# A retention layer that feeds a token-mixing layer on one core: instructions put in another order, three more transposes by DMA, and sums in two PSUM banks at the end

## The chip, the core and the metric

The kernel runs on one core of a Trainium2 chip. That core has five engines, each of which works through its own list of instructions in order: TensorE (PE in the profile; PEld is its loading of weights), VectorE (DVE), ScalarE (ACT), GpSimd (POOL) and SyncE (SP, which issues the DMA transfers here). They wait for each other through semaphores. Matrix products are written to PSUM, a memory in banks, from which DVE and ACT read them here. The metric is the device time of one execution in microseconds (us).

## The reference, cut to what matters

```python
# retention: q, k, v of [4 batches, 8 heads, 768 tokens, 64]
for t in range(S):
    state = gamma[None, :, None, None] * state + np.einsum('bhd,bhe->bhde', k[:, :, t], v[:, :, t])
    y[:, :, t] = scale * np.einsum('bhd,bhde->bhe', q[:, :, t], state)
x = np.ascontiguousarray(attn_out.transpose(0, 2, 1, 3)).reshape(B, S, H * D)   # [4, 768, 512]
# mixing
theta = x @ w_theta
cos_t, sin_t = (np.cos(theta), np.sin(theta))
zr = x * cos_t
zi = x * sin_t
yr = np.einsum('ts,bsd->btd', w_tok_r, zr)
yi = np.einsum('ts,bsd->btd', w_tok_i, zi)
y = yr + yi
u = x + y
return (u + np.maximum(u @ w_ch, 0.0))
```

## The kernel before, in words

**Tiles.** The 768 tokens of a batch are six tiles of 128. The retention takes them two at a time: a *pair* n (0 to 11, three to a batch) covers 256 tokens as two interleaved chunks of 128. The mixing takes the 24 tiles one at a time and calls them m (0 to 23, six to a batch).

**A pair.** `prep` scales and casts k (ACT), q and v (POOL, in the first pairs partly DVE) to bf16. `flip` turns k and q round with eight PE transposes each into one PSUM bank, and DVE copies that bank out (L186); `flip_dma` does the same by one DMA transpose. `ret_A` multiplies k and q, `ret_mask` masks the product (DVE, L211), `ret_Y` multiplies it with v, `ret_I` adds the part that comes from the state. `ret_S` adds k and v to the state in PSUM and ends with two ACT copies that put the state into `stbd` for the next `ret_I` (L266). `ret_out` copies the pair's x, still transposed, out of PSUM (two ACT copies, L275). `x_pe` or `x_dma` turns x round. `theta` makes x @ w_theta for one chunk (four PE matmuls) and lets ACT take cosine and sine (L299, L300); `zmul` multiplies both with x (DVE, L306).

**A tile.** `moe_M` sums twelve matmuls, two for each of six steps s0 (step s0 needs z of chunk s0 of the batch), into one bank `y_ps`. `moe_u` adds x to it (DVE, L325). `moe_U` (PE transposes, ACT copy) or `moe_U_dma` turns u round, `moe_O` makes u @ w_ch (four matmuls), `moe_out` finishes (DVE, L353), `store` writes out.

**PSUM banks** are handed out by tag: `y` has one bank, `tr` two (all transposes and `o_ps` in turn), `acc` two (the two `yT_ps` of a pair, then the two `th_ps`, and so on in turn), `at` and `st` hold the masked product and the state. A new user of a bank waits until its last reader is through.

**Order.** Nothing is scheduled by a planner: `manual_schedule` leaves each engine's instructions in the order in which the code is written. A prologue (L441 to L537) handles pairs 0 to 2, with `keep_busy` matmuls that do no work of the reference. Then *slot* n = 3 to 12 (L547 on) does the first half of pair n, the second half of pair n - 1, the tiles `tiles_of[n]` (one tile in slots 3 to 6, two from slot 7 on), and the `moe_O` of the slot before. `w_cast` and `w_tok` cast and transpose one row block of the token weights. After slot 12 come tiles 18 to 22 one by one, and `moe_last` for tile 23.

**Loads.** SP issues the loads of pairs 0 to 5 and all weights at the start, in the order of L111, as buffers come free. The loads of pair n + 3 are issued in slot n, in SP's order behind what stands before them: `x_dma`, `flip_dma`, `moe_U_dma` and the stores are issued by SP too.

**What the change touches.** In `ret_S` the state copies (L264 to L266). In the slot: the DMA limit for k and q (`KQ_DMA`, L63 and L550), the places of `moe_U_dma` (L556), `w_cast(4)` (L565), `theta` and `x_pe` (L586 to L589), the split of the first tile's products at `part` (L583), the flips (L593), `w_tok` (L600, L619), and the order of `moe_M`, `moe_u`, `zmul` and `moe_O` at the slot's end (L612 to L628). The tag of `y_ps` (L314), the last lines of the prologue and the loop of the last tiles.

Of the kernel before, what the change touches and what calls it, by code (L numbers as in the profile page):

```python
# [14 lines left out]
FT = mybir.dt.float32  # L15
# [17 lines left out]
def kernel(  # L33
# [18 lines left out]
    B, H, S, D = q.shape  # L52
    dm = H * D
# [191 lines left out]
    def ret_S(n, a):  # L245

        b, g = divmod(n, nG)
        c = 2 * g + a
        if c == nT - 1:
            return  # L250
        half = slice(a * HP, (a + 1) * HP)
        if c == 0:
            st_ps[b] = psum.tile([P, NP, D], FT, name="st_ps", tag="st", bufs=1)
        for two in range(2):
            for j in range(NP):
                for par in range(2):
                    h = 2 * j + par
                    nc.tensor.matmul(st_ps[b][par * D:(par + 1) * D, j, :],  # L258
                                     st[n, "k"][half, two, h * D:(h + 1) * D],
                                     st[n, "v"][half, two, h * D:(h + 1) * D],  # L260
                                     start=(c == 0 and two == 0 and j == 0),
                                     stop=(c == nT - 2 and two == 1 and j == NP - 1),
                                     skip_group_check=True)
        for par in range(2):  # L264
            sl = slice(par * D, (par + 1) * D)
            nc.scalar.copy(stbd[(c + 1) % 2][sl, :, sl], st_ps[b][sl])  # L266
# [184 lines left out]
    ret_mask(0, 0)  # L451
    keep_busy(2)
    ret_S(0, 0)
    keep_busy(1)
    ret_A(0, 1)
    ret_mask(0, 1)
    ret_S(0, 1)
    ret_Y(0, 0)
    ret_I(0, 1)
    keep_busy(3)  # L460
# [16 lines left out]
    ret_mask(1, 0)  # L477
    keep_busy(2)
    ret_S(1, 0)
    ret_A(1, 1)  # L480
    ret_mask(1, 1)
    prep(2, "k", K)
    ret_Y(1, 0)
    ret_I(1, 0)
    ret_S(1, 1)
    ret_I(1, 1)
    keep_busy(2)
    zmul(0, 0)
# [16 lines left out]
    theta(1, 1)  # L505
    x_pe(1, 1, 2)
    ret_S(2, 0)
    ret_A(2, 1)
    ret_mask(2, 1)
    ret_Y(2, 0)  # L510
# [24 lines left out]
    flip(3, "q")  # L535
    prep(4, "k", K)
    w_cast(3)  # L537


    tiles_of = {nG - 2: [], nG - 1: [0, 1]}  # L540
# [6 lines left out]
    for n in range(nG, B * nG + 1):  # L547
        mine, done = tiles_of[n], tiles_of[n - 1]
        late, two = n > nG, len(mine) > 1
        q_dma = n + 1 >= KQ_DMA  # L550
# [9 lines left out]
        if n + 1 in pairs:  # L560
            prep(n + 1, "q", PP)
            prep(n + 1, "v", PP)
        if n == nG:
            nc.gpsimd.tensor_copy(wch, wdma["ch"])
            w_cast(4)  # L565
        if n == nG + 1:
            w_cast(5)
        if late:
# [24 lines left out]
        if n + 1 in pairs:  # L593
            if q_dma:
                flip_dma(n + 1, "q")
            else:
                flip(n + 1, "k")
                flip(n + 1, "q")
        if n == nG:
            w_tok(3)  # L600
        if n + 3 in pairs:
            load(n + 3, "v")
        for t in tiles_of[n - 2]:
            store(t)

        if n in pairs:
            ret_S(n, 0)
            ret_A(n, 1)
            ret_mask(n, 1)
            ret_Y(n, 0)  # L610
            ret_I(n, 0)
        if n < U_DMA:  # L612
            moe_U(done)
        if two:
            moe_M(mine[1], 0, nT)
        else:
            moe_M(mine[0], part, nT)
        if n in (nG, nG + 1):
            w_tok(n - nG + 4)  # L619
# [12 lines left out]
    for m in range(last_m - nT + 1, last_m):  # L632
        if m - 1 > last_m - nT:
            moe_U_dma(m - 1)
        else:
            moe_U_dma(m - 2)
            moe_U_dma(m - 1)
        moe_M(m, 0, nT)
        moe_u(m)
# [8 lines left out]
_INS = ['q', 'k', 'v', 'moe_w_theta', 'moe_w_tok_r', 'moe_w_tok_i', 'moe_w_ch']  # L648
# [26 lines left out]
```

## Time and profile before

| what | value |
|---|---|
| time, median of 13 runs | 180.96 us (180.09 to 183.65) |
| time of the profiled execution | 180.96 us |
| its span | 179.3 us |
| PE busy | 162.5 us, 91% of the span |
| DVE, ACT, POOL busy | 103.7, 82.7, 63.2 us |
| read from HBM, written to it | 25.69 MB, 6.29 MB |

The span is the stretch from the first to the last instruction; the 1.7 us between it and the time lie outside of what the profile shows. A line of the profile gives a start in us from the span's start and a duration. In square brackets stands how long the engine had been idle before that instruction, and what ended the wait. A matmul's row is longer than its share of the engine, since the next one starts while it drains; so a short wait of PE shows less idle time than it costs. In this trace, slots 3 to 12 begin at about 43.3, 53.6, 65.1, 75.5, 84.3, 95.5, 107.7, 118.6, 129.9 and 141.2 us, and the last tiles at 151.4.

### The profile page before, as it was taken

Reading aid. Unit: us, or ns where it says so; the run is one execution under the profiler, and the core shown is the slowest. Engines: PE = TensorE matmul, PEld = TensorE weight load, DVE = VectorE, ACT = ScalarE, POOL = GpSimd, SP = SyncE. Lnnn points to the kernel's source line nnn. Section 1 sums busy time; section 2 is a strip of 40 time slices with the busy share of each in tenths; the row PEclk is TensorE's granted clock in tenths of the full one; section 3 lists DMA queues with packets and bytes.
Section 4 is the critical chain, followed back from the end, with each engine's and each line's share of the span. In section 5 each row is a group of like instructions: output and inputs, shape, how many; then the busy total and the mean of one; then the engine's idle time right before and its main releaser. Section 6 shows DMA issues by size and latency. Waiting matters only on the chain.

```text
span 179.3 us, 4745 instructions
## 1 busy us (share of the span) xinstructions
PE 162.5 (91%) x2003; PEld 90.3 (50%) x2003; DVE 103.7 (58%) x142; ACT 82.7 (46%) x141; POOL 63.2 (35%) x81
## 2 busy tenths in 40 slices
PE   7689898977798997999999999999999989999990
PEld 2355565544544654655465645454455434444560
DVE  2366798775644674969297474672746535334441
ACT  7236494932356658575773744728055250000010
POOL 5284656492996856802718063000000000000000
PEclk9999999999999999999999999999999999999999
DMA  4999999999999999339696596765719162353343
GB/s 137 311 328 332 295 316 331 347 343 282 321 335 295 291 305 314 122 65 286 162 252 185 120 263 124 200 119 102 165 29 208 29 176 58 138 148 100 88 146 119
DMA packets 63621, 37.13 MB, mean 207 GB/s; under 512 B 20976, under 2 KB 58096, under 8 KB 63600
## 3 DMA queue, kind: packets, MB, share of 16 engines
q1 hardware_dynamic: 63456, 36.71, 76.0%
q8 instruction: 15, 0.25, 0.6%
q10 hardware_dynamic: 144, 0.13, 0.2%
q14 instruction: 6, 0.05, 0.1%
HBM read 25.69 MB, written 6.29 MB: 178 GB/s over the span
## 4 chain that ended last, share of the span: by engine, by line
PE 67%; ACT 8%; DMA 8%; DVE 6%; issue 5%; POOL 3%; DVEq 0%; ACTq 0%; POOLq 0%
PE y_ps L318 27%; PE o_ps L346 11%; PE th_ps L296 10%; DMA pair<-in_q_dram 6%; PE kq_ps L183 3%; PE yT_ps L227 3%; ACT cs L300 3%; PE at_ps L204 3%; PE yT_ps L241 3%; DMA pair<-in_k_dram 2%; PE st_ps L258 2%; ACT cs L299 2%; PE y_ps L392 2%; DVE z L306 1%; DVE at L211 1%
## 5 line engine op out<-in xcount | busy, mean ns | idle before, releaser
L318 PE MATMUL y_ps<-z,wtr 128*128 128x512 bf16 x138 | 52.4, 380 | 1.5 <-DVE u L325 1.0
L318 PE MATMUL y_ps<-z,wti 128*128 128x512 bf16 x138 | 52.4, 379 | 0.0
L325 DVE TENSOR_TENSOR u<-y_ps,x_sb 128x512 bf16<-128x512 f32 x23 | 15.9, 690 | 39.7 <-PE y_ps L318 39.6
L175 POOL TENSOR_TENSOR kqb<-pair,qscp 128x512 bf16<-128x512 f32 x20 | 22.0, 1115 | 38.1 <-DMA pair<-in_q_dram 31.0
L211 DVE TENSOR_TENSOR at<-at_ps,maskp 128x1024 bf16<-128x1024 f32 x24 | 29.3, 1220 | 4.1 <-PE at_ps L204 4.1
L266 ACT CAST stbd<-st_ps 64x256 bf16<-64x256 f32 x40 | 14.6, 365 | 27.2 <-PE st_ps L258 26.7
L175 POOL TENSOR_TENSOR kqb<-pair,vscp 128x512 bf16<-128x512 f32 x24 | 25.4, 1079 | 3.6 <-DMA pair<-in_v_dram 1.9
L296 PE MATMUL th_ps<-wth,xT 128*128 128x512 bf16 x96 | 23.2, 380 | 1.4 <-ACT xT L275 1.3
L346 PE MATMUL o_ps<-wch,uT 128*128 128x512 bf16 x92 | 22.8, 379 | 0.3 <-DVE wtr L378 0.3
L318 PEld LDWEIGHTS <-wti 128*128 128x128 bf16 x138 | 13.5, 98 | 16.0 <-issue 3.1
L299 ACT ACTIVATE cs<-th_ps,halfpi 128x512 bf16<-128x512 f32 x24 | 16.5, 689 | 10.1 <-PE th_ps L296 10.1
L318 PEld LDWEIGHTS <-wtr 128*128 128x128 bf16 x138 | 13.4, 97 | 14.4
L275 ACT CAST xT<-yT_ps 128x512 bf16<-128x512 f32 x22 | 15.0, 737 | 11.1 <-PE yT_ps L227 10.9
L186 DVE COPY kqT<-kq_ps 128x1024 bf16<-128x1024 bf16 x20 | 13.5, 687 | 9.2 <-PE kq_ps L183 9.0
L353 DVE SCALAR_TENSOR_TENSOR ot<-o_ps,u 128x512 f32<-128x512 f32 x23 | 15.9, 691 | 4.8 <-PE o_ps L346 4.6
L306 DVE TENSOR_TENSOR z<-cs,x_sb 128x1024 bf16<-128x1024 bf16 x24 | 17.6, 772 | 0.5 <-DMA x_sb<-xT 0.4
L300 ACT ACTIVATE cs<-th_ps,zerob 128x512 bf16<-128x512 f32 x24 | 16.5, 688 | 0.0
L183 PE MATMUL kq_ps<-ident,kqb 128*128 128x128 bf16 x160 | 11.8, 219 | 4.0 <-DVE kqb L175 1.0
L169 ACT CAST kqb<-pair 128x1024 bf16<-128x1024 f32 x12 | 12.6, 1048 | 5.5 <-DMA pair<-in_k_dram 5.4
L296 PEld LDWEIGHTS <-xT 128*128 128x128 bf16 x96 | 8.6, 97 | 12.4 <-ACT xT L275 3.7
L346 PEld LDWEIGHTS <-uT 128*128 128x128 bf16 x92 | 8.9, 97 | 10.7 <-issue 0.7
L183 PEld LDWEIGHTS <-kqb 128*128 128x128 bf16 x160 | 9.9, 98 | 7.7 <-issue 2.4
(57 smaller groups left out, 155.7 us busy)
## 6 DMA issues: line engine op xcount, KB each, us to landing
pair<-in_k_dram SPq DMA_DIRECT2D x12, 512.0 KB, 6.7
pair<-in_q_dram SPq DMA_DIRECT2D x12, 512.0 KB, 7.6
pair<-in_v_dram SPq DMA_DIRECT2D x12, 512.0 KB, 8.0
out_dram<-ot SPq DMA_DIRECT2D x23, 256.0 KB, 2.6
wtok<-in_moe_w_tok_r_dram SPq DMA_DIRECT2D x6, 384.0 KB, 6.5
wtok<-in_moe_w_tok_i_dram SPq DMA_DIRECT2D x6, 384.0 KB, 6.3
w<-in_moe_w_theta_dram SPq DMA_DIRECT2D x1, 1024.0 KB, 8.1
w<-in_moe_w_ch_dram SPq DMA_DIRECT2D x1, 1024.0 KB, 8.9
```

What stands on the lines that cost most here:

```text
L175: engines[two].tensor_mul(dst[:, two], src[:, two], _bcast_last(sc[:, 2 * g + two], D))
L183: nc.tensor.transpose(ps[:, two, j, :], st[n, name][:, two, j * P:(j + 1) * P], ident)
L211: nc.vector.tensor_mul(at.rearrange("p a j t -> p (a j) t"), at_ps.rearrange("p a j t -> p (a j) t"), _bcast_mid(maskp[:, two].rearrange(" ...
L275: copy(st[n, "xT"][:, a].rearrange("e j (i w) -> e j w i", w=2), st[n, "y"][a].rearrange("e j (w i) -> e j w i", w=2))
L296: nc.tensor.matmul(th_ps, st[n, "xT"][:, a, j, :], wth[:, j, :], start=(j == 0), stop=(j == NP - 1))
L299: nc.scalar.activation(cs[:, 0, :], th_ps, AF.Sin, bias=halfpi, scale=1.0)
L300: nc.scalar.activation(cs[:, 1, :], th_ps, AF.Sin, bias=zerob, scale=1.0)
L306: nc.vector.tensor_mul(zs[b][:, c], st[n, "cs", a], _bcast_mid(xs[b][:, c, :], 2))
L318: nc.tensor.matmul(y_ps, wT[r][:, s0, t0 * P:(t0 + 1) * P], zs[b][:, s0, r, :], start=(s0 == 0 and r == 0), stop=(s0 == nT - 1 and r == 1))
L325: nc.vector.tensor_add(u, mo[m]["y"], xs[b][:, t0, :])
L346: nc.tensor.matmul(o_ps, mo[m]["uT"][:, j, :], wch[:, j, :], start=(j == 0), stop=(j == nD - 1))
L353: nc.vector.scalar_tensor_tensor(ot, mo[m]["o"], 0.0, mo[m]["u"], ALU.max, ALU.add)
```

## The change

- **State copies.** They leave `ret_S` and become `state_out`. Everywhere but in one place it is called right behind `ret_S`, so nothing moves there. In the slot, for pair n - 1, it is called behind the two `ret_out`.
- **k by DMA.** `flip` of k becomes `flip_dma` for pairs 7, 8 and 9 too (slots 6, 7 and 8); q stays with PE up to pair 9.
- **Products.** The first of two tiles is split after three steps in place of four, around the two `theta`. Of a single tile the steps 2 and 3 come before the `w_tok`, the steps 4 and 5 behind it (in slot 6 the steps 2 and 3 come right behind the flip). `x_pe` stands between the two `theta`.
- **u.** The `moe_u` of a single tile comes before `zmul`. From slot 8 on, the first tile's `moe_U_dma` is issued in its own slot.
- **Weights.** `w_tok(2)` and `w_tok(3)` move up in the prologue, the second from slot 3; `flip(3, "k")`, `flip(3, "q")` stand inside products; `w_cast(4)` goes ahead of the cast of w_ch on POOL.
- **The end.** From tile 17 on `y_ps` takes the two banks of `acc` in turn. In slot 12 the second tile comes behind both `moe_O`; in tiles 18 to 22 `moe_O` stands between the steps 3 and 4.

```diff
-    KQ_DMA, X_DMA, U_DMA = 3 * nG + 1, 2 * nG - 1, 3 * nG
+    K_DMA, Q_DMA, X_DMA, U_DMA = 2 * nG + 1, 3 * nG + 1, 2 * nG - 1, 3 * nG
...
+    def state_out(n, a):
+        b, g = divmod(n, nG)
+        c = 2 * g + a
+        if c == nT - 1:
+            return
         for par in range(2):
             sl = slice(par * D, (par + 1) * D)
             nc.scalar.copy(stbd[(c + 1) % 2][sl, :, sl], st_ps[b][sl])
...
-            mo[m] = dict(y=psum.tile([P, dm], FT, name="y_ps", tag="y", bufs=1))
+            if m < (B - 1) * nT - 1:
+                y_ps = psum.tile([P, dm], FT, name="y_ps", tag="y", bufs=1)
+            else:
+                y_ps = psum.tile([P, dm], FT, name="y_ps", tag="acc", bufs=2)
+            mo[m] = dict(y=y_ps)
...
     moe_M(0, 2, 4)
     zmul(2, 0)
     prep(3, "k", K)
+    w_tok(2)
+    moe_M(0, 4, 5)
     zmul(2, 1)
-    moe_M(0, 4, nT)
+    flip(3, "k")
+    moe_M(0, 5, nT)
     moe_u(0)
     prep(3, "q", DP)
     prep(3, "v", PP)
-    w_tok(2)
-    flip(3, "k")
-    moe_M(1, 0, nT)
+    w_cast(3)
+    moe_M(1, 0, 4)
+    flip(3, "q")
+    moe_M(1, 4, nT)
     moe_u(1)
-    flip(3, "q")
+    w_tok(3)
     prep(4, "k", K)
-    w_cast(3)
...
-        if n + 1 in pairs and q_dma:
+        nxt = n + 1 in pairs
+
+        if nxt and n + 1 >= K_DMA:
             flip_dma(n + 1, "k")
         if n + 3 in pairs:
             load(n + 3, "k")
         if n >= U_DMA:
-            for t in done:
-                moe_U_dma(t)
+            moe_U_dma(done[1])
...
             ret_S(n - 1, 1)
             ret_out(n - 1, 0, nc.scalar.copy)
             ret_out(n - 1, 1, nc.scalar.copy)
+            state_out(n - 1, 1)
...
-        part = 4 if two else 2
-        moe_M(mine[0], 0, part)
+        first = mine[0]
+        moe_M(first, 0, 3 if two else 2)
         if late:
             theta(n - 1, 0)
-            theta(n - 1, 1)
             if n - 1 < X_DMA:
                 x_pe(n - 1)
+            theta(n - 1, 1)
         if two:
-            moe_M(mine[0], part, nT)
-            moe_u(mine[0])
...
+            moe_M(first, 3, nT)
+            moe_u(first)
+        for name, limit in (("k", K_DMA), ("q", Q_DMA)):
+            if nxt and n + 1 < limit:
+                flip(n + 1, name)
+        if not two and n + 1 >= K_DMA:
+            moe_M(first, 2, 4)
+        if nxt and n + 1 >= Q_DMA:
+            flip_dma(n + 1, "q")
...
+        if n + 1 >= U_DMA:
+            moe_U_dma(first)
...
-        if two:
+        if not two:
+            if n + 1 < K_DMA:
+                moe_M(first, 2, 4)
+            if n in (nG, nG + 1):
+                w_tok(n - nG + 4)
+            moe_M(first, 4, nT)
+            moe_u(first)
+        elif n in pairs:
             moe_M(mine[1], 0, nT)
...
         if late:
             zmul(n - 1, 0)
             zmul(n - 1, 1)
-        moe_u(mine[-1])
+        if two and n in pairs:
+            moe_u(mine[1])
         for t in done:
             moe_O(t)
             moe_out(t)
+        if n not in pairs:
+            moe_M(mine[1], 0, nT)
+            moe_u(mine[1])
...
     for m in range(last_m - nT + 1, last_m):
...
+        moe_U_dma(m - 1)
+        moe_M(m, 0, 4)
...
         moe_O(m - 2)
         moe_out(m - 2)
         store(m - 2)
+        moe_M(m, 4, nT)
+        moe_u(m)
```

Three places show what this does to the engines' lists. The first is ACT's list around slot 4, before the change; `xT` are the two x copies, `stbd` the state copies, `cs` cosine and sine.

```order
L169 CAST kqb<-pair 128x1024
L266 CAST stbd_174<-st_ps 64x4x64 x2
L275 CAST xT<-yT_ps 128x4x2x64 x2
L299 ACTIVATE cs<-th_ps,halfpi 128x512
L300 ACTIVATE cs<-th_ps,zerob 128x512
```

And the same place after it (line numbers are those of the changed code):

```order
L169 CAST kqb<-pair 128x1024
L281 CAST xT<-yT_ps 128x4x2x64 x2
L272 CAST stbd_174<-st_ps 64x4x64 x2
L305 ACTIVATE cs<-th_ps,halfpi 128x512
L306 ACTIVATE cs<-th_ps,zerob 128x512
```

The x copies, for which `theta` waits on PE, now stand ahead of the state copies.

The second is DVE's list from the middle of slot 5 to the middle of slot 6, before; `z` are the two `zmul` of a pair, `u` and `ot` the two DVE steps of a tile, `kqT` the copies of flipped k and q.

```order
L211 TENSOR_TENSOR at<-at_ps,maskp 128x1024
L306 TENSOR_TENSOR z<-cs,x_sb 128x1024 x2
L325 TENSOR_TENSOR u<-y_ps,x_sb 128x512
L353 SCALAR_TENSOR_TENSOR ot<-o_ps,u 128x512
L211 TENSOR_TENSOR at<-at_ps,maskp 128x1024
L186 COPY kqT<-kq_ps 128x1024 x2
```

And after:

```order
L211 TENSOR_TENSOR at<-at_ps,maskp 128x1024
L335 TENSOR_TENSOR u<-y_ps,x_sb 128x512
L312 TENSOR_TENSOR z<-cs,x_sb 128x1024 x2
L363 SCALAR_TENSOR_TENSOR ot<-o_ps,u 128x512
L211 TENSOR_TENSOR at<-at_ps,maskp 128x1024
L186 COPY kqT<-kq_ps 128x1024
```

`u`, which sets the bank `y` free, has moved ahead of `z`, and one of the two `kqT` copies is gone.

The third is SP's list from slot 6 to the start of slot 7, before; `pair` are loads, `x_sb` is `x_dma`.

```order
L81 DMA pair<-in_k_dram 128x8x128
L280 DMA_TRANSPOSE x_sb<-xT 128x8x128
L81 DMA pair<-in_q_dram 128x8x128
L81 DMA pair<-in_v_dram 128x8x128
L358 DMA out_dram<-ot 128x512
```

And after:

```order
L191 DMA_TRANSPOSE kqT<-kqb 128x8x128
L81 DMA pair<-in_k_dram 128x8x128
L286 DMA_TRANSPOSE x_sb<-xT 128x8x128
L81 DMA pair<-in_q_dram 128x8x128
L81 DMA pair<-in_v_dram 128x8x128
L368 DMA out_dram<-ot 128x512
```

The transpose of k, which cannot be issued before ACT has cast that k, stands ahead of the slot's loads.

More of the change, by code (lines that the diff above doesn't have):

```diff
@@ L453 @@
     ret_S(0, 0)
+    state_out(0, 0)
     keep_busy(1)
@@ L457 @@
     ret_S(0, 1)
+    state_out(0, 1)
     ret_Y(0, 0)
@@ L479 @@
     ret_S(1, 0)
+    state_out(1, 0)
     ret_A(1, 1)
@@ L485 @@
     ret_S(1, 1)
+    state_out(1, 1)
     ret_I(1, 1)
@@ L507 @@
     ret_S(2, 0)
+    state_out(2, 0)
     ret_A(2, 1)
@@ L549 @@
         late, two = n > nG, len(mine) > 1
-        q_dma = n + 1 >= KQ_DMA
-        if n + 1 in pairs and q_dma:
+        nxt = n + 1 in pairs
+        if nxt and n + 1 >= K_DMA:
             flip_dma(n + 1, "k")
@@ L556 @@
         if n >= U_DMA:
-            for t in done:
-                moe_U_dma(t)
-        if n + 1 in pairs:
+            moe_U_dma(done[1])
+        if nxt:
             prep(n + 1, "q", PP)
@@ L563 @@
         if n == nG:
+            w_cast(4)
             nc.gpsimd.tensor_copy(wch, wdma["ch"])
-            w_cast(4)
         if n == nG + 1:
@@ L582 @@
             load(n + 3, "q")
-        part = 4 if two else 2
-        moe_M(mine[0], 0, part)
+        first = mine[0]
+        moe_M(first, 0, 3 if two else 2)
         if late:
             theta(n - 1, 0)
-            theta(n - 1, 1)
             if n - 1 < X_DMA:
                 x_pe(n - 1)
+            theta(n - 1, 1)
         if two:
-            moe_M(mine[0], part, nT)
-            moe_u(mine[0])
[L593 to L600, printed above, removed]
+            moe_M(first, 3, nT)
[7 more added lines that the diff above has]
+            flip_dma(n + 1, "q")
         if n + 3 in pairs:
@@ L604 @@
             store(t)
+        if n + 1 >= U_DMA:
+            moe_U_dma(first)
         if n in pairs:
             ret_S(n, 0)
+            state_out(n, 0)
             ret_A(n, 1)
@@ L613 @@
             moe_U(done)
-        if two:
+        if not two:
[6 more added lines that the diff above has]
+        elif n in pairs:
             moe_M(mine[1], 0, nT)
[L616 to L619, printed above, removed]
         if n + 2 in pairs:
@@ L628 @@
             moe_out(t)
+        if n not in pairs:
+            moe_M(mine[1], 0, nT)
+            moe_u(mine[1])
     last_m = B * nT - 1
     for m in range(last_m - nT + 1, last_m):
[L633 to L639, printed above, removed]
+        moe_U_dma(m - 1)
+        moe_M(m, 0, 4)
         if m == last_m - nT + 1:
```

## The prediction

> **What bounds the kernel now.** I first cut the span into the slots of the code and asked for the busy time of each engine in them. The columns are the stretch, its length, and for each engine the busy time and number of instructions; behind POOL stand the clock granted to PE, the DMA engines' share and GB/s.
>
> ```profile
> 43.30:53.60 10.30, 8.99 (x132) 5.60 (x132) 6.14 (x8) 4.11 (x6) 9.69 (x10) 1.00 1.08 321
> 53.60:65.10 11.50, 10.22 (x169) 6.53 (x168) 6.39 (x9) 6.98 (x14) 7.67 (x9) 1.00 1.15 303
> 65.10:75.50 10.40, 9.39 (x157) 5.82 (x156) 7.69 (x10) 7.39 (x13) 8.70 (x8) 1.00 0.85 242
> 75.50:84.30 8.80, 8.45 (x130) 5.07 (x129) 7.20 (x10) 5.88 (x10) 0.07 (x2) 1.00 0.59 144
> 84.30:95.50 11.20, 11.20 (x162) 6.58 (x161) 7.38 (x10) 6.75 (x12) 6.07 (x6) 1.00 0.86 236
> 107.70:118.60 10.90, 10.77 (x126) 5.37 (x125) 6.31 (x9) 5.40 (x9) 1.56 (x2) 1.00 0.74 167
> 129.90:141.20 11.30, 11.17 (x146) 5.77 (x145) 6.33 (x9) 5.08 (x10) 0.00 (x0) 1.00 0.51 94
> 141.20:151.40 10.20, 9.42 (x61) 4.36 (x60) 3.92 (x7) 3.74 (x6) 0.00 (x0) 1.00 0.40 104
> ```
>
> These are slots 3, 4, 5, 6, 7, 9, 11 and 12. From slot 4 on no engine but PE comes near its stretch's length: PE is the bound, and in slot 7 it has no gap at all. So time is won there in two ways only, by fewer PE instructions or by fewer PE gaps. Slot 3 is different: POOL is busy 9.69 of 10.30 us and the DMA engines are full. What does PE wait for there? The timeline of POOL, then of PE:
>
> ```profile
> 43.91 2.04 POOL L175 TENSOR_TENSOR kqb<-pair,qscp 128x512 bf16<-128x512 f32 x2 [3.51 <-DMA pair<-in_q_dram]
> 47.90 1.89 POOL L564 CAST wch<-w 128x2048 bf16<-128x2048 f32 x1
> 49.73 1.60 POOL L365 CAST wrow<-wtok 128x768 bf16<-128x768 f32 x2
> ```
> ```profile
> 38.70 0.60 PE L183 MATMUL kq_ps<-ident,kqb 128*128 128x128 bf16 x8 [0.89 <-ACT wti L376]
> 43.28 0.42 PE L204 MATMUL at_ps<-kqT 64*64 64x128 bf16 x16 [0.93 <-DVE kqT L186]
> 46.01 0.40 PE L183 MATMUL kq_ps<-ident,kqb 128*128 128x128 bf16 x4 [0.60 <-POOL kqb L175]
> 51.77 1.02 PE L346 MATMUL o_ps<-wch,uT 128*128 128x512 bf16 x4
> ```
>
> POOL gets the q of pair 4 at 43.91, after 3.51 us of waiting for its load. PE needs that q at 46.01 (flip of q) and waits for it. From 43.91 POOL works without a pause: q, v, w_ch, two weight rows, to 49.73 + 1.60 = 51.33. So up to 46.01 the loads set the pace, and up to 51.33 POOL does.
>
> **The price of a wait.** The row of a 512-column matmul is about 0.38 us long, but the next starts after 0.86 / 4 = 0.215 us:
>
> ```profile
> 89.04 0.86 PE y_ps L318 x4
> 89.91 0.89 PE kq_ps L183 x16
> ```
>
> So a wait behind such a matmul costs the idle time shown plus some 0.16 us that its draining covers. The second row is two flips: 0.445 us of PE each.
>
> **Prologue and slot 3.** Two waits of the prologue, 0.89 and 0.93 us (with draining 2.1 us), get other work into them: flips stand inside products, `w_tok` moves up. I count this at nothing. PE comes earlier to the flip of pair 4's q, and that q still comes when its load lands; no load is moved. Behind it, slot 3 loses `w_tok(3)`, but its `moe_O` needs w_ch, which POOL now casts last: 43.91 + 2 x 2.04 + 1.60 + 1.89, with the same overlaps, is again 51.33. The first `moe_O` can start at 51.38 in place of 51.77: **0.4 us**. PE itself is there in time: from the end of the flip, 46.01 + 4 x 0.056 = 46.23 (0.89 / 16 = 0.056 us a transpose), it took 5.54 us to 51.77, and twelve transposes, 0.67 us, now leave this stretch; so it comes at 51.1 at the latest.
>
> **Slots 4 and 5: state copies, x_pe, w_tok, u.** The waits of PE in slots 4, 5 and the start of 6, from its timeline:
>
> ```profile
> 56.45 1.90 PE L296 MATMUL th_ps<-wth,xT 128*128 128x512 bf16 x8 [0.63 <-ACT xT L275]
> 59.58 0.61 PE L183 MATMUL kq_ps<-ident,kqb 128*128 128x128 bf16 x8 [0.34 <-DVE x_sb L290]
> 64.27 1.02 PE L346 MATMUL o_ps<-wch,uT 128*128 128x512 bf16 x4 [0.31 <-DVE wtr L378]
> 67.98 1.90 PE L296 MATMUL th_ps<-wth,xT 128*128 128x512 bf16 x8 [0.67 <-ACT xT L275]
> 71.11 0.61 PE L183 MATMUL kq_ps<-ident,kqb 128*128 128x128 bf16 x8 [0.34 <-DVE x_sb L290]
> 76.72 0.38 PE L318 MATMUL y_ps<-z,wtr 128*128 128x512 bf16 x1 [0.25 <-DVE u L325]
> ```
>
> And ACT in slot 4:
>
> ```profile
> 54.89 0.76 ACT L266 CAST stbd<-st_ps 64x256 bf16<-64x256 f32 x2 [1.21 <-PE st_ps L258]
> 55.67 1.33 ACT L275 CAST xT<-yT_ps 128x512 bf16<-128x512 f32 x2
> ```
>
> - *State copies.* Without them in front the x copies start 55.67 - 54.89 = 0.78 us earlier, and `theta` can start at 56.45 - 0.78 = 55.67, which is when PE ends the four products before it (56.45 - 0.63 - 0.16 = 55.66). Both `theta` waits go: 0.79 and 0.83 us. The state is read again only by `ret_I` behind `ret_A` and `ret_Y` of the same slot; what is late next is cosine and sine, which start after the state copies.
> - *x_pe between the thetas.* The second flip waits for the bank that DVE frees after `x_pe`. Now 0.86 us of `theta` lies between: both waits of 0.34 + 0.16 go, 0.50 us each.
> - *w_tok(5) inside products.* The wait for DVE's copy, 0.31 + 0.16, is covered by 0.86 us of products: 0.47 us.
> - *Next in line.* `ret_Y` of the slot's pair reuses the banks of `theta` and waits for the last sine. From the end of the second `theta` ACT needs its two last rows of some 0.7 us (such a row stands below), while PE has two flips, 0.89 us, and the short matmuls of `ret_S` and `ret_A`. The two are about equal; I take nothing off, and keep some tenths a slot for the range.
>
> Together 1.76 us in slot 4 and 1.33 in slot 5.
>
> **Slot 6.** The wait at 76.72 is for u, which stood behind z on DVE:
>
> ```profile
> 73.51 2.55 DVE L306 TENSOR_TENSOR z<-cs,x_sb 128x1024 bf16<-128x1024 bf16 x2
> 75.98 0.68 DVE L325 TENSOR_TENSOR u<-y_ps,x_sb 128x512 bf16<-128x512 f32 x1
> ```
>
> With u first it is done before PE asks for the bank: 0.25 + 0.16 = 0.41 us. Off that goes 0.1, my estimate for x: its first copy takes 1.33 / 2 = 0.67 us behind `ret_Y`, hardly less than the four products of 0.86 that cover it. 0.3 net. z moves back by one row, 0.68 us; it is used a slot later. The flip of k goes: 0.445 us. And slots 6, 9, 10 and 11 have a shorter wait, which no bracket shows:
>
> ```profile
> 76.07 0.40 PE L227 MATMUL yT_ps<-at,kqb 64*64 64x128 bf16 x16
> 80.79 0.73 PE L227 MATMUL yT_ps<-at,kqb 64*64 64x128 bf16 x16
> 113.55 0.76 PE L227 MATMUL yT_ps<-at,kqb 64*64 64x128 bf16 x16
> 113.15 0.70 ACT L300 ACTIVATE cs<-th_ps,zerob 128x512 bf16<-128x512 f32 x1
> ```
>
> `ret_Y` takes 0.33 to 0.36 us longer there than undisturbed, until the last sine ends (113.85). Two or four more products now stand between `theta` and `ret_Y`, 0.43 us or more. So 0.33 in slot 6, 1.08 us in all there.
>
> **Slots 7 to 11.** Slots 7 and 8 have no gap to close and lose a flip each: 0.89 us. In 9 to 11 the `ret_Y` wait goes; slots 9 and 11 show the same 0.13 us of idle, and I take 0.34 three times: 1.02 us. Cover left: 0.43 against 0.34, so 0.1.
>
> **Slot 12 and the end.** The wait for the one bank `y`, then the chain's rows of the last tiles:
>
> ```profile
> 145.96 0.38 PE L318 MATMUL y_ps<-z,wti 128*128 128x512 bf16 x1
> 147.12 0.38 PE L318 MATMUL y_ps<-z,wtr 128*128 128x512 bf16 x1 [0.78 <-DVE u L325]
> ```
> ```profile
> 151.60 2.59 PE y_ps L318 x12
> 154.19 0.86 PE o_ps L346 x4
> 155.05 2.67 PE y_ps L318 x12
> ```
>
> From 145.96 + 0.215 to 147.12 are 0.94 us; `moe_O` and another bank fill them. A tile's products take 2.67 in place of 2.59 us, because they wait for u: 0.08 for five tiles, 0.40. Together 1.34 us.
>
> **The DMA transposes.** What PE saves is paid on SP and the DMA engines:
>
> ```profile
> kqT<-kqb SPq DMA_TRANSPOSE x4, 3.4
> ```
> ```profile
> 73.60 1.05 ACT L169 CAST kqb<-pair 128x1024 bf16<-128x1024 f32 x1
> 92.69 1.05 ACT L169 CAST kqb<-pair 128x1024 bf16<-128x1024 f32 x1
> ```
> ```profile
> 69.11 0.39 SPq L81 DMA_DIRECT2D pair<-in_k_dram  x1
> ```
>
> k of pair 7 is cast by 74.65 and would land at 78.1; slot 7 needs it at 84.3, so 6 us are left. SP waits for that cast; behind it stands the load of pair 9's k, issued at 69.11 before and now some 7 us later. ACT casts that k only at 92.69. The q, v and stores behind it already waited for x. `moe_U_dma` of a first tile only comes earlier. I count zero; a landing 6 us late would be the point from which it costs.
>
> **The sum.** 0.4 + 1.76 + 1.33 + 1.08 + 0.89 + 1.02 + 1.34 = 7.8 us. The profiled execution took 180.96 us, which is also the median of the runs. **180.96 - 7.8 = 173.1 us.**
>
> **The rivals.**
>
> - *The loads don't hold it.* If the 2.1 us of the prologue counted too: 171.0 us. For it speaks that they are real PE gaps; against it the 3.51 us of POOL idle before pair 4's q. Chance 0.06.
> - *A new wait.* `ret_Y` waits for cosine and sine in slots 4 to 11 after all, or x_pe's copy is late behind other DVE work; of the 3.1 us in slots 4 and 5, the 1.08 in 6 and the 1.02 after, half comes back: 175.7 us. For it: margins of a few tenths. Chance 0.16.
> - *Loads or POOL bind on to slot 6.* Then 180.96 - 0.4 - 0.89 - 1.02 - 1.34 = 177.3 us. For it: POOL's 8.70 of 10.40 us in slot 5 and full DMA engines. Against it: POOL is idle in slot 6 (0.07 us), since it runs a slot ahead. Chance 0.05.
> - *The clock of PE falls.* Sums that go from bank to bank could bring the granted clock down in the last stretch, some 24 us of PE work without a gap from 151 on. At half clock for all of it that costs 24 us; a third of it eats the 7.8, and half gives 173.1 + 12 = 185 us: slower. Against it: the clock is 1.00 in every row above, and `yT_ps`, `th_ps` and `o_ps` change banks in all of them. Chance 0.02.
>
> The Trainium skill's page "TensorE: Matmul & The Clock Gate" states such a rule (section "A second HAM failure mode: psum-queue depth-cycling"): PE that cycles through PSUM banks pauses so often that its clock swings between half and full rate. The rows disagree for this kernel, since banks alternate there at a granted clock of 1.00; by the page alone the time would be this rival's.
>
> **How the numbers follow.** My forecast has 0.69, and the other 0.02 is for no gain from causes that I don't see. A measurement of this kernel tells about 0.3%, 0.54 us, from no change. Every case but the last two is faster by more: 0.96 faster, 0.02 same, 0.02 slower. The range goes from the first rival, 171.0, widened by nothing, to the second, 175.7; outside lie the third and fourth and some of the edges.
>
> **What would show it.** Right: the brackets at `theta`, at the second flip, at `moe_O` of slot 4 and at the second tile of slot 12 are gone; slots 6 to 8 have eight `kq_ps` transposes each in place of 16; tiles 18 to 22 take 3.45 us each; `moe_O` of slot 3 starts near 51.4, with PE idle before pair 4's q. Wrong: POOL's q of pair 4 earlier than 43.9; a wait of `ret_A` for a DMA in slots 7 to 9; a clock under 1; or a slot 3 that ends later than 53.6.

## The result, and the profile after

The changed kernel takes **172.29 us** (median of 11 runs, 171.74 to 173.63; the three longest, from 172.99 on, had a mean granted clock of 0.987 to 0.989, the others 0.997 or more). Over the whole study the kernel before takes 181.14 us (median of 48 runs, 180.09 to 183.65). The ratio is 0.9518, with a 95% interval of 0.9496 to 0.954: 8.7 us less, between 8.3 and 9.1. In what follows a difference between two kernels that were timed against the kernel before is the difference of their ratios times 181 us; "by its slots" means read from the profiles, as the difference of the starts of the slots' first matmuls.

The same stretches as before, slot by slot; the columns are again the stretch, its length, then busy time and instructions of each engine, PE's granted clock, the DMA share and GB/s.

```profile
43.30:53.36 10.06, 7.71 (x103) 4.24 (x101) 5.24 (x7) 4.41 (x6) 9.19 (x9) 1.00 1.04 312
53.36:63.13 9.77, 9.77 (x170) 6.59 (x169) 6.19 (x10) 7.30 (x13) 7.12 (x9) 1.00 0.96 279
63.13:72.22 9.09, 9.09 (x157) 5.92 (x156) 7.30 (x11) 6.92 (x13) 5.19 (x6) 1.00 1.07 314
...
79.97:90.71 10.74, 10.74 (x153) 6.15 (x152) 7.30 (x10) 6.62 (x13) 4.74 (x5) 1.00 1.21 258
...
134.87:166.11 31.24, 31.24 (x177) 15.46 (x176) 12.96 (x21) 4.12 (x7) 0.00 (x0) 1.00 0.45 126
```

These are slots 3, 4, 5 and 7, and the stretch from slot 12 to the last `moe_O`. From slot 4 on, PE's busy time is the whole length of each stretch (of those left out too): it shows no gap in any of them, where before only slots 7 and 8 had none. Slot 3 still shows POOL at 9.19 of 10.06 us and DMA engines that are full. The two timelines there, POOL's and PE's:

```profile
44.17 2.04 POOL L175 TENSOR_TENSOR kqb<-pair,qscp 128x512 bf16<-128x512 f32 x2 [4.32 <-DVE at L211]
...
49.69 1.89 POOL L582 CAST wch<-w 128x2048 bf16<-128x2048 f32 x1
```
```profile
46.27 0.40 PE L183 MATMUL kq_ps<-ident,kqb 128*128 128x128 bf16 x4 [0.60 <-POOL kqb L175]
...
51.64 1.89 PE L356 MATMUL o_ps<-wch,uT 128*128 128x512 bf16 x8 [0.46 <-POOL wch L582]
```

POOL still stands idle for 4.32 us before pair 4's q, though PE comes earlier now, and the first `moe_O` still waits for POOL, at 51.64 in place of 51.77. (The profile names the mask as the releaser, which ended at 44.10. The q itself landed at 44.04 by the trace, 0.13 us before POOL's start; where the profile does name the load, POOL starts as close behind it, at 46.31 after a landing at 46.17 in the last profile below.) Then slot 4, from PE's timeline:

```profile
55.38 1.03 PE L302 MATMUL th_ps<-wth,xT 128*128 128x512 bf16 x4
56.24 0.61 PE L295 MATMUL x_ps<-ident,xT 128*128 128x128 bf16 x8
56.69 1.03 PE L302 MATMUL th_ps<-wth,xT 128*128 128x512 bf16 x4
57.55 1.06 PE L183 MATMUL kq_ps<-ident,kqb 128*128 128x128 bf16 x16
```

No square brackets: neither `theta` nor the second flip waits, and the starts follow each other at 0.86, 0.45, 0.86 us. The last tiles on the chain of waits:

```profile
150.48 2.59 PE y_ps L328 x12
153.07 0.86 PE o_ps L356 x4
153.93 2.59 PE y_ps L328 x12
```

A tile takes 3.45 us; its products no longer show the 0.08 us behind a shared bank.

### The profile page after: what moved, and what is told of

Same layout as the page of the kernel before. It is cut to its first block, busy times and chain, and to the rows that moved or that the text cites. A ratio compares the mean times of both kernels' runs of the same rounds, so it can differ in the third digit from the quotient of the medians.

```text
span 170.6 us, 4701 instructions
## 1 busy us (share of the span) xinstructions
PE 158.8 (93%) x1979; PEld 88.3 (52%) x1979; DVE 102.2 (60%) x139; ACT 82.5 (48%) x141; POOL 63.2 (37%) x81
## 4 chain that ended last, share of the span: by engine, by line
PE 80%; DVE 5%; ACT 4%; POOL 4%; DMA 2%; issue 2%; DVEq 0%
PE y_ps L328 33%; PE th_ps L302 12%; PE o_ps L356 12%; PE kq_ps L183 4%; PE at_ps L204 4%; PE yT_ps L227 3%; PE yT_ps L241 3%; PE st_ps L258 3%; DMA pair<-in_k_dram 2%; DVE at L211 2%; POOL kqb L175 2%; ACT kqb L169 2%; PE y_ps L402 2%; DVE kqT L186 1%; PE w_ps L382 1%
## 5 line engine op out<-in xcount | busy, mean ns | idle before, releaser
L175 POOL TENSOR_TENSOR kqb<-pair,qscp 128x512 bf16<-128x512 f32 x20 | 21.4, 1087 | 34.1 <-DMA pair<-in_q_dram 20.6
L312 DVE TENSOR_TENSOR z<-cs,x_sb 128x1024 bf16<-128x1024 bf16 x24 | 18.5, 810 | 0.1
L186 DVE COPY kqT<-kq_ps 128x1024 bf16<-128x1024 bf16 x17 | 11.5, 687 | 11.7 <-PE kq_ps L183 11.7
L183 PE MATMUL kq_ps<-ident,kqb 128*128 128x128 bf16 x136 | 10.3, 220 | 3.5 <-ACT kqb L169 1.2
L414 ACT COPY uT<-u_ps 128x256 bf16<-128x256 bf16 x2 | 0.7, 372 | 25.6 <-PE u_ps L413 25.6
```

The lines of the kernel that those rows point to most:

```text
L175: engines[two].tensor_mul(dst[:, two], src[:, two], _bcast_last(sc[:, 2 * g + two], D))
L183: nc.tensor.transpose(ps[:, two, j, :], st[n, name][:, two, j * P:(j + 1) * P], ident)
L312: nc.vector.tensor_mul(zs[b][:, c], st[n, "cs", a], _bcast_mid(xs[b][:, c, :], 2))
```

## The experiments

**State copies alone.** The kernel before, with nothing but this:

```diff
...
-            ret_S(n - 1, 1)
+            ret_S(n - 1, 1, False)
             ret_out(n - 1, 0, nc.scalar.copy)
             ret_out(n - 1, 1, nc.scalar.copy)
+            state_out(n - 1, 1)
```

> The kernel before with one edit: in the slot the two state copies of pair n - 1 come behind the two x copies on ACT. My theory: the two waits of theta in slots 4 and 5 (0.79 and 0.83 us in the profile of before) go and nothing takes their place, so 1.6 us less than before, about 179.5 us, with both brackets at theta gone and the 0.34 us brackets at the second flip still there. Rival: the cosine and sine chain on ACT, which starts behind the state copies, is late instead and ret_Y takes the wait over: less than 0.5 us gained.

Measured: 179.25 us, ratio 0.9874 (0.983 to 0.9919), 2.3 us less (1.5 to 3.1). Its `theta` rows of slots 4 and 5:

```profile
56.23 1.89 PE L304 MATMUL th_ps<-wth,xT 128*128 128x512 bf16 x8
66.91 1.89 PE L304 MATMUL th_ps<-wth,xT 128*128 128x512 bf16 x8
```

The waits of 0.63 and 0.67 us are gone. By its slots slot 4 is 0.81 and slot 5 0.84 us shorter, 1.65 together, and no later slot moves. (Slot 3 ends 0.57 us later in this profile.) The rest of the 2.3 lies in the stretch behind the last products (below) and in the uncertainty.

**The converse: all of the change but this.** The changed kernel with the state copies in front of the x copies again.

```diff
             ret_S(n - 1, 1)
+            state_out(n - 1, 1)
             ret_out(n - 1, 0, nc.scalar.copy)
             ret_out(n - 1, 1, nc.scalar.copy)
-            state_out(n - 1, 1)
```

> The changed kernel with the state copies in front of the x copies again in the slots (all else of it kept). Theory (only slots 4 and 5 waited for the x copies): theta waits some 0.8 us again in slots 4 and 5, where four products cover the x copies, and not from slot 6 or 7 on, where six or more do; +1.6 us against the changed kernel. Rival A (three steps in place of four leave no cover in the later slots either): a theta wait in slots 7 to 11 as well, +0.2 us or more each, +2.5 us or more in all. Rival B (x_pe between the two theta hides it): below +0.5 us. The last store's issue on ACT's queue should stay at 0.37 us and the drain at 4.5 us if they belong to the order of the end.

Measured: 175.8 us, ratio 0.9694 (0.9656 to 0.9732), 3.2 us more than the changed kernel: twice what I expected, and what rival A said. `theta` waits in slots 4, 5, 7, 8, 10 and 11; the rows of slots 4, 7, 10 and 11:

```profile
56.51 1.04 PE L302 MATMUL th_ps<-wth,xT 128*128 128x512 bf16 x4 [0.64 <-ACT xT L281]
...
84.77 1.90 PE L302 MATMUL th_ps<-wth,xT 128*128 128x512 bf16 x8 [0.21 <-ACT xT L281]
...
118.62 1.90 PE L302 MATMUL th_ps<-wth,xT 128*128 128x512 bf16 x8 [0.20 <-ACT xT L281]
129.98 1.25 PE L302 MATMUL th_ps<-wth,xT 128*128 128x512 bf16 x5 [0.26 <-ACT xT L281]
```

Slots 4 and 5 are 0.81 and 0.85 us longer than in the changed kernel, slots 7, 8, 10 and 11 by 0.38, 0.44, 0.37 and 0.43 (the idle time shown and the 0.16 of the draining matmul). Slots 6 and 9 don't move: there pair n - 1 is the last of a batch, and its second chunk has no state copies. So three steps ahead of `theta` are enough only because the state copies went away; with four steps (in the kernel before) 0.43 us more of products covered them. Two edits that I had priced apart need each other: undone in one order, the state copies are worth 1.65 us, in the other 3.28.

**The split.** The changed kernel, split after four steps as before:

```diff
-        moe_M(first, 0, 3 if two else 2)
+        moe_M(first, 0, 4 if two else 2)
...
-            moe_M(first, 3, nT)
+            moe_M(first, 4, nT)
```

> The changed kernel with one edit: the first of two tiles is split after four steps again. My theory: ret_Y waits for the last sine again in slots 9, 10 and 11, 0.34 us each, and not in slots 7 and 8, where the flip of q covers it: 1.0 us slower than the changed kernel. Rival: that wait is set by something else (the mask on DVE), and nothing changes.

Measured: 174.02 us, ratio 0.9594 (0.9554 to 0.9635), 1.4 us more than the changed kernel. Slots 9, 10 and 11 are 0.36, 0.38 and 0.38 us longer, 1.1 in all; slots 7 and 8 don't move (10.74 and 11.83 us). Its chain of waits in slot 10:

```profile
115.98 0.88 PE th_ps L302 x4
117.46 0.68 ACT cs L306
118.14 0.58 ACT cs L305
118.72 0.59 ACT cs L306
```

The chain leaves PE behind the first `theta` and runs through ACT's cosines and sines until `ret_Y` may start. This is the wait of slots 9 to 11 that no bracket shows. In slots 7 and 8 PE still flips q between `theta` and `ret_Y`, 0.445 us, and that is cover enough.

**k by PE again.** The changed kernel with k of pairs 7 to 9 flipped on PE:

```diff
-        if nxt and n + 1 >= K_DMA:
+        if nxt and n + 1 >= Q_DMA:
             flip_dma(n + 1, "k")
...
-        for name, limit in (("k", K_DMA), ("q", Q_DMA)):
+        for name, limit in (("k", Q_DMA), ("q", Q_DMA)):
```

> The changed kernel with k of pairs 7, 8 and 9 flipped by PE again, in front of q. My theory: eight transposes in each of slots 6, 7 and 8 come back on a PE without gaps, 0.445 us each, so 1.3 us slower than the changed kernel. Rival: the three DMA transposes cost about what they save, because they stand in front of the loads in SP's list and share the DMA engines: no difference, or a little faster with PE.

Measured: 173.54 us, ratio 0.9585 (0.9545 to 0.9625), 1.2 us more. Slot 7 on its chain of waits:

```profile
87.18 0.89 PE kq_ps L183 x16
```

Sixteen transposes in 0.89 us again, as in slots 6 and 8; slots 6, 7 and 8 are 0.45 us longer each and no other slot from 4 on moves. (Slot 3 ends 1.1 us later in this profile, since pair 4's q came 1.0 us later; the clock fell there too, as the last section shows.) What the DMA transposes take from SP and from the DMA engines costs nothing that these runs can see. In the changed kernel they take longer from issue to landing, and no matmul waits for one:

```profile
kqT<-kqb SPq DMA_TRANSPOSE x7, 4.1
```

4.1 us is the median of seven, 3.1 to 5.7; before it was 3.4. The 6 us that were left for them held.

**Two banks alone.** The kernel before with `y_ps` of tiles 17 on in the two banks of `acc`, and nothing else:

```diff
-            mo[m] = dict(y=psum.tile([P, dm], FT, name="y_ps", tag="y", bufs=1))
+            if m < (B - 1) * nT - 1:
+                y_ps = psum.tile([P, dm], FT, name="y_ps", tag="y", bufs=1)
+            else:
+                y_ps = psum.tile([P, dm], FT, name="y_ps", tag="acc", bufs=2)
+            mo[m] = dict(y=y_ps)
```

> The kernel before with one edit: from tile 17 on the sums take the two acc banks in turn; the order is that of before. My theory: the wait at tile 17 (0.94 us) and five waits of 0.08 us go, so 1.3 us less than before by PE, about 179.8 us. The changed kernel also ended 0.9 us sooner behind its last matmul (last store landing earlier), which no term of mine holds. If that belongs to the banks or the order at the end, this run shows it too and gains 2.2 us; if it comes and goes by itself, it is not tied to this edit. Rival, by the clock: banks in turn bring the granted clock below 1.00 and the run is slower.

Measured: 180.19 us, ratio 0.9935 (0.9904 to 0.9965), 1.2 us less (0.6 to 1.7). The stretch from slot 12 to the last `moe_O`, and a tile on the chain:

```profile
141.83:173.21 31.38, 31.32 (x178) 15.56 (x176) 13.15 (x21) 4.12 (x7) 0.00 (x0) 1.00 0.45 126
```
```profile
154.76 2.59 PE y_ps L322 x12
```

31.38 us against 32.65 before, at a granted clock of 1.00.

**One bank with the new order.** The changed kernel with every `y_ps` in bank `y`:

```diff
-            if m < (B - 1) * nT - 1:
+            if m < B * nT:
```

> The changed kernel with all sums in the one bank y again, the new order kept. My theory: with moe_O inside a tile's products nothing stands between the last product of a tile and the first of the next, so each of the six changes of tile from 17 on waits for u, 0.94 us as at tile 17 in the profile of before: 5.6 us slower than the changed kernel. So the two banks carry the order, and not the order the gain. Rival: u is hidden as before, and it costs 0.1 us a tile, 0.5 us in all.

Measured: 178.31 us, ratio 0.9841 (0.9801 to 0.9881), 5.8 us more. One turn of its chain, from u to u:

```profile
158.92 0.70 DVE u L335
159.67 1.89 PE y_ps L328 x8
161.56 0.86 PE o_ps L356 x4
162.42 0.88 PE y_ps L328 x4
163.32 0.70 DVE u L335
```

`moe_O` now stands inside a tile's products, so nothing lies between the last product of one tile and the first of the next: each tile waits for DVE's u, 4.40 us a turn in place of 3.45. The order of the last tiles is bought with the second bank; with one it would be worse than the old order.

**The prologue put back.** The changed kernel with the prologue and `w_tok(3)` of the kernel before:

```diff
-    w_tok(2)
-    moe_M(0, 4, 5)
     zmul(2, 1)
-    flip(3, "k")
-    moe_M(0, 5, nT)
+    moe_M(0, 4, nT)
     moe_u(0)
     prep(3, "q", DP)
     prep(3, "v", PP)
-    w_cast(3)
-    moe_M(1, 0, 4)
-    flip(3, "q")
-    moe_M(1, 4, nT)
+    w_tok(2)
+    flip(3, "k")
+    moe_M(1, 0, nT)
     moe_u(1)
-    w_tok(3)
+    flip(3, "q")
     prep(4, "k", K)
+    w_cast(3)
...
+        if n == nG:
+            w_tok(3)
```

> The changed kernel with the last lines of the prologue put back (w_tok(2), both flips of pair 3 and w_cast(3) where they were, w_tok(3) in slot 3 again). My theory: slot 3 is held by pair 4's q (landing near 44 us) and then by POOL up to the cast of w_ch, so the prologue's waits cost nothing: within 0.3 us of the changed kernel, with the first o_ps of slot 3 again near 51.6 us. Rival: the waits of 0.89 and 0.93 us in the prologue and the transposes in slot 3 count, and it is 2 us slower than the changed kernel.

Measured: 172.83 us, ratio 0.9536 (0.949 to 0.9582), 0.3 us more than the changed kernel, which is within the uncertainty of some 0.9 us. The two PE waits of 0.89 and 0.93 us are back, where the changed kernel's PE waits 0.95 us for u at 38.58 and 0.52 us for pair 4's k at 44.28. POOL starts that pair's q when it lands, here too:

```profile
43.87 2.04 POOL L175 TENSOR_TENSOR kqb<-pair,qscp 128x512 bf16<-128x512 f32 x2 [3.53 <-DMA pair<-in_q_dram]
```

So the prologue's part of the change is worth nothing that this measurement can tell, as it must be if the loads pin slot 3.

**Pair 4 loaded ahead of w_ch.** If that is so, moving the load must move the time. The changed kernel with one word of the list of loads moved:

```diff
-    loads("p0 th p1 w0 p2 w1 w2 p3 w3 ch p4 w4 p5 w5")
+    loads("p0 th p1 w0 p2 w1 w2 p3 w3 p4 ch w4 p5 w5")
```

> The changed kernel with one edit in the order of the loads: pair 4 ahead of w_ch. My theory (loads hold slot 3, then POOL): q of pair 4 lands about 3 us sooner, near 41 us, so PE's wait for it goes; POOL then waits for the token weights (landing near 47 and 48 us, not moved), casts them by 48.9 and w_ch by 50.8. The first o_ps of slot 3 starts near 50.8 in place of 51.6: 0.85 us faster than the changed kernel. Rival: PE or DVE work of the prologue sets the start, and the loads' order changes nothing.

Measured: 171.67 us, ratio 0.9468 (0.9438 to 0.9498), 0.9 us less than the changed kernel (0.2 to 1.6). POOL's list:

```profile
40.75 2.04 POOL L175 TENSOR_TENSOR kqb<-pair,qscp 128x512 bf16<-128x512 f32 x2 [1.69 <-DMA pair<-in_q_dram]
46.74 0.82 POOL L375 CAST wrow<-wtok 128x768 bf16<-128x768 f32 x1 [1.95 <-DMA wtok<-in_moe_w_tok_r_dram]
48.70 1.89 POOL L582 CAST wch<-w 128x2048 bf16<-128x2048 f32 x1
```

q is there 3.4 us earlier; then POOL waits for the weight rows, and w_ch, the last of its list, ends 1.0 us earlier than in the changed kernel. The first `moe_O` starts at 50.65, also 1.0 us earlier. Slot 5 of this profile takes 0.48 us of it back: its second flip waits 0.37 us for DVE's copy of x, at 67.30.

**And w_ch's cast ahead of the weight rows.** On top of that, w_ch is cast before `w_cast(4)`, `prep(4, "k")` stands ahead of `w_tok(3)`, and `w_tok(4)` behind slot 3's `moe_O`:

```diff
-    w_tok(3)
     prep(4, "k", K)
+    w_tok(3)
...
-            w_cast(4)
             nc.gpsimd.tensor_copy(wch, wdma["ch"])
+            w_cast(4)
...
-            if n in (nG, nG + 1):
-                w_tok(n - nG + 4)
+            if n == nG + 1:
+                w_tok(5)
...
+        if n == nG:
+            w_tok(4)
```

> The changed kernel with pair 4 loaded ahead of w_ch, the cast of w_ch ahead of w_cast(4) on POOL again, the cast of pair 4's k ahead of w_tok(3), and w_tok(4) behind the two moe_O of slot 3. My theory: then neither the load of q nor the token weights stand before moe_O; w_ch lands near 45.8, is cast by 47.8, and the first o_ps starts there, with w_tok(4) after it slot 4 begins near 50.7 in place of 53.4. That is 2.6 us faster than the changed kernel, near 169.7 us, if the later loads still come in time (by their landings they have 1 to 3 us to spare). Rival: the loads bind again in slots 4 and 5, the waits move there, and less than 1 us is left.

Measured: 170.82 us, ratio 0.9426 (0.939 to 0.9462), 1.7 us less than the changed kernel; I had expected 2.6. The profiled run, 172.0 us, is the longest of its six, so its trace shows less gain than the median. The PE waits of slots 3 and 4:

```profile
48.90 1.89 PE L356 MATMUL o_ps<-wch,uT 128*128 128x512 bf16 x8 [0.98 <-POOL wch L581]
51.57 0.49 PE L382 MATMUL w_ps<-ident,wrow 128*128 128x128 bf16 x6 [0.37 <-DVE ot L363]
54.74 1.04 PE L302 MATMUL th_ps<-wth,xT 128*128 128x512 bf16 x4 [0.66 <-ACT xT L281]
```

`moe_O` starts 2.7 us earlier, and then `theta` of slot 4 waits again, for a new reason: ACT's list has the k of pair 5 ahead of the x copies, and that k had not landed. This wait and the one before it cost 0.82 and 0.53 us with the draining matmuls, and 0.67 us of the 2.7 are no gain, since the twelve transposes of `w_tok(4)` have only moved behind `moe_O`. So slot 5 begins 0.63 us earlier in this profile. Its w_ch started on POOL at 46.96, behind its load, and at 45.94 in the next profile, which has the same list of loads.

```profile
52.31 1.04 ACT L169 CAST kqb<-pair 128x1024 bf16<-128x1024 f32 x1 [5.07 <-DMA pair<-in_k_dram]
53.95 1.33 ACT L281 CAST xT<-yT_ps 128x512 bf16<-128x512 f32 x2
```

**k of pair 5 cast by POOL.** On top of that again, so that ACT waits for no load there, and `w_tok(4)` behind slot 4's first products:

```diff
+        if n == nG + 1:
+            w_tok(4)
...
-            prep(n + 2, "k", K)
+            prep(n + 2, "k", (nc.gpsimd,) if n == nG else K)
...
-        if n == nG:
-            w_tok(4)
```

> The kernel with the loads of pair 4 and w_ch's cast ahead, with k of pair 5 cast by POOL in place of ACT, and w_tok(4) put in slot 4 behind its first products. Theory (the loads set the pace of slot 3 and, once that is mended, of slot 4 through ACT, which waits for the k of pair 5 ahead of the x copies): the wait at theta in slot 4 (0.66 us) and the one of w_tok(4) (0.37 us) go, 0.8 to 1.4 us less than with the loads and w_ch alone, near 169.9 us. Rival (by then the DMA engines hold everything up to slot 5, whatever engine casts): no gain over it, 170.8 us, with the wait at another place of slots 4 or 5.

Measured: **169.98 us**, ratio 0.9381 (0.934 to 0.9422), 0.8 us less than without it, which is no more than the uncertainty of some 1.0 us, and 2.5 less than the changed kernel, which is clear of it: the fastest median of the study. The profile shows what became of the waits. PE's two `theta` of slot 4, and the only wait that its timeline shows from slot 4 on:

```profile
52.29 1.03 PE L302 MATMUL th_ps<-wth,xT 128*128 128x512 bf16 x4
53.60 1.03 PE L302 MATMUL th_ps<-wth,xT 128*128 128x512 bf16 x4
65.02 0.61 PE L183 MATMUL kq_ps<-ident,kqb 128*128 128x128 bf16 x8 [0.18 <-DVE x_sb L296]
```

**The end alone.** The kernel before with the two banks (their lines stand above) and with `moe_O` of tiles 18 to 22 inside their products, slot 12 in its old order. The reason to run it is a stretch that I had not priced. These are the last stores of the kernel before, then of the changed kernel, as issued on ACT's queue:

```profile
173.83 1.24 PE L422 MATMUL o_ps<-wch,uT 128*128 128x256 bf16 x8
...
175.67 1.17 ACTq L429 DMA_DIRECT2D out_dram<-oh  x1
```
```profile
166.11 1.24 PE L432 MATMUL o_ps<-wch,uT 128*128 128x256 bf16 x8
...
167.96 0.37 ACTq L439 DMA_DIRECT2D out_dram<-oh  x1
```

The same instructions with the same work take 179.25 - 173.83 = 5.42 us from the last matmuls to the end of the span before, and 170.57 - 166.11 = 4.46 after; 0.8 us of the difference is the issue, 1.17 in place of 0.37 us.

```diff
-        moe_M(m, 0, nT)
-        moe_u(m)
+        moe_M(m, 0, 4)
...
         moe_O(m - 2)
         moe_out(m - 2)
         store(m - 2)
+        moe_M(m, 4, nT)
+        moe_u(m)
```

> The kernel before with the sums of tiles 17 to 23 in two banks and with moe_O of tiles 18 to 22 between the steps 3 and 4 of the tile's products; slot 12 in its old order. Theory (the shorter drain behind the last products comes with the order of the last tiles): PE gains 1.3 us as with the two banks alone, and the drain from the last moe_O to the end takes 4.5 us in place of 5.4, with the last store's issue on ACT's queue at 0.37 us: -2.2 us. Rival (the drain differs from run to run in the old order and the new alike): -1.3 us, and a drain anywhere from 4.5 to 5.4 us.

Measured: 179.96 us, ratio 0.9935 (0.9902 to 0.9969), 1.2 us less (0.6 to 1.8). Its stretch from slot 12 to the last `moe_O` takes 31.15 us, 1.50 less than before, but:

```profile
174.63 0.87 ACTq L433 DMA_DIRECT2D out_dram<-oh  x1
```

The drain takes 5.1 us. So the order of the last tiles alone does not bring the short drain.

**The kernel before, once more.** One more profile of it:

> The kernel before once more, for its profile: if the long drain at the end belongs to its order, the last store's issue on ACT's queue is again well over 0.37 us and the drain near 5.4 us; if it differs from run to run, either may be short.

Measured: 183.94 us, one run; issue 0.87 us, drain 5.1 us. Over all profiles the drain is 5.42, 5.1, 5.1, 5.1 and 4.6 us where slot 12 has its old order (the last with the state copies moved), and 4.45 to 4.63 in nine profiles where it has the new one; the issue 0.87 to 1.17 us in four of the five and 0.37 or 0.38 in all nine. It was long in both profiles of the kernel before, so it goes more with the kernel than with the run; which part of a kernel decides stays open, for the one with the state copies alone has the old order and a short issue.

This profile shows something else as well. Pair 4's q came 2.4 us later than in the first profile of the same kernel:

```profile
46.31 2.04 POOL L175 TENSOR_TENSOR kqb<-pair,qscp 128x512 bf16<-128x512 f32 x2 [6.36 <-DMA pair<-in_q_dram]
```

The flip behind it came 2.4 us later, the first `moe_O` 3.7 us later (55.48 in place of 51.77), and from slot 4 on the slots have their old lengths, but for a slot 6 that is 0.27 us shorter. One late load moved the whole rest of the program.

## Why the prediction was right, point by point

Predicted were 173.1 us and 7.8 us of gain; measured 172.29 and 8.7. The gains by slots, before less after, beside the terms of the sum:

| term | predicted | by the slots |
|---|---|---|
| slot 3 (w_ch cast last) | 0.4 | 0.28 |
| slot 4 (theta, x_pe, w_tok) | 1.76 | 1.72 |
| slot 5 (theta, x_pe) | 1.33 | 1.29 |
| slot 6 (u, k, `ret_Y`) | 1.08 | 1.02 |
| slots 7, 8 (k) | 0.89 | 0.89 |
| slots 9 to 11 (`ret_Y`) | 1.02 | 1.11 |
| slot 12 and the last tiles | 1.34 | 1.41 |
| from the last matmuls to the end | 0 | 0.96 |
| sum | 7.8 | 8.7 |

- **The price of a wait** (idle time shown plus 0.16 us) held: the brackets of 0.63 and 0.67 us were worth 0.81 and 0.84, those of 0.20 to 0.26 us 0.37 to 0.44.
- **PE as the bound from slot 4 on** held: all PE terms together are 7.7 us against 7.8. Nothing new became late. Cosine and sine, the likeliest rival, do run close: four steps in place of three bring 1.1 us of waits back in slots 9 to 11.
- **The prologue at nothing** held: put back, it costs 0.3 us, within the uncertainty. The rival in which the loads don't hold it falls, and with pair 4 loaded earlier the time falls by 0.9 us.
- **Slot 3 was mis-sized**, 0.28 in place of 0.4 us: the sum on POOL takes q's start as fixed at 43.91, and in this profile it was 44.17, so w_ch's cast ended at 51.58 and not at 51.33. Starts of this kind vary by more than that from run to run (43.12 to 46.31 us in the eleven profiles with this order of loads).
- **The DMA transposes at zero** held: k by PE costs 1.2 us, and the transposes land later than before without anybody waiting.
- **The two banks** held, at 1.41 for 1.34 us. The sum put 0.94 on slot 12 and 0.40 on the tiles; the banks alone, in the old order, already bring 1.27 by the slots and the order of the tiles another 0.2. What I had not seen is that the new order needs them, 5.8 us with one bank.
- **The missing term** is the end of the program. The sum stopped at PE's last matmul. Of the 0.96 us there, the profiles of the old order give between 0.2 and 1.0, so some of it is the one profile that I started from. It is the largest part of why 172.29 is below 173.1.
- **The clock** stayed at 1.00 with sums that change banks, in the profiles of the changed kernel and of the two banks alone: the products that alternate take 2.59 us a tile, less than the 2.67 in one bank. What the Trainium skill's page "TensorE: Matmul & The Clock Gate", section "A second HAM failure mode: psum-queue depth-cycling", reports of another kernel, that PE cycling through banks pauses so often that its clock swings, is not seen here. In the profiles of this study in which the clock fell while PE had work, it fell in slot 3, far from these sums (last section); for the three longest runs of the changed kernel no trace shows where.
- **One step was too simple**, without harm to the sum: I priced the state copies (0.79 and 0.83 us) and the split after three steps (0.34 a slot) as if each stood alone. With the split but without the state copies moved, slots 7, 8, 10 and 11 wait 1.62 us more.

## What to carry to other kernels

Price a wait as its idle time plus what the draining instruction in front of it hides, and look for waits without a bracket by comparing the same group's length in a stretch where nothing delays it. Cover that one edit uses up may be what another edit frees, so undo each part from the changed kernel as well as doing it alone. When one engine has no gaps left, look at where its first stretch is pinned: here the order of the loads and the casts behind them gave another 2.5 us, each step showing the next wait.

## What the runs showed of the hardware

- The same store by the same instruction took 0.37 us to issue on ACT's queue in some kernels and 0.87 or 1.17 in others, at the same place of the program.
- In three profiles PE waited in slot 3 for a late q of pair 4, and then its granted clock fell to 0.50. PE's rows around the fall in the second profile of the kernel before, then in the changed kernel with k by PE again:

```profile
45.83:49.25 3.42, 1.13 (x14) 0.84 (x15) 0.93 (x2) 0.00 (x0) 2.94 (x3) 1.00 1.10 336
49.25:52.66 3.41, 3.08 (x62) 2.71 (x63) 1.97 (x3) 1.43 (x3) 3.41 (x4) 0.50 0.96 240
```
```profile
43.88:47.29 3.41, 1.12 (x14) 0.71 (x14) 1.09 (x2) 0.59 (x1) 2.14 (x3) 1.00 1.06 342
47.29:50.70 3.41, 3.41 (x62) 2.68 (x63) 1.92 (x2) 1.15 (x3) 3.41 (x5) 0.50 1.14 295
```

  In the third, the changed kernel with one bank, PE was busy for 1.83 of 3.42 us, and the clock was 0.50 from 48.18 to 51.59. Each fall lasted 3.41 us. These are the three profiles in which POOL started that q at 45.15 us or later; in the other eleven, with 44.50 or earlier, slot 3 kept 1.00. In the kernel before, the fall is where the 1.3 us come from by which the first `moe_O` was later than the load explains, as far as one profile can tell. In the other two the first `moe_O` came 1.13 and 1.34 us later than in the changed kernel for a q that came 0.98 and 1.10 us later, so there the fall cost some 0.2 us at most.

  The Trainium skill's page "TensorE: Matmul & The Clock Gate", section "HAM oscillation — how this bites in real kernels", sums it up as no idle gaps of PE over some 3.4 us. Here the longest idle time that a bracket shows before a fall was 1.79, 1.11 and 0.93 us, so much shorter waits were enough where they came close together. The share of busy time alone does not decide it: in the prologue of the kernel with the two banks alone PE was busy for less than in the third profile, 1.64 of 3.41 us, and the clock stayed at 1.00.

```profile
34.87:38.28 3.41, 1.64 (x7) 0.58 (x6) 2.93 (x3) 1.84 (x3) 3.41 (x3) 1.00 1.03 371
38.28:41.70 3.42, 2.53 (x27) 1.74 (x26) 2.85 (x4) 1.25 (x2) 1.03 (x2) 1.00 1.18 299
```

- The transposes of k and q by DMA landed after 3.1 to 5.7 us in the changed kernel, where the first of them share slots 6 to 8 with loads (DMA share 1.04 to 1.25), and after 3.1 to 4.7 in the kernel before, which has them only from slot 9 on.
